# First token block of a fused attention and MoE kernel: matmuls in float32 on the decoded weights, splits moved to the second block

## The chip, the cores and the metric

The kernel runs on one core of a Trainium2 chip. The metric is device time in microseconds (us) of one launch. Engines are named as in the profile: PE is TensorE, DVE is VectorE, ACT is ScalarE, POOL is GpSimd, SP is SyncE, which only issues the DMAs.

## The reference

The attention's inputs are float32; the MoE weights come as float64 and are decoded to float32 on the chip. Cut to what matters:

```python
# attention: B=8, H=8, S=576, D=64, pool=8
k_p = k.reshape(B, H, Sp, pool, D).mean(axis=3)
v_p = v.reshape(B, H, Sp, pool, D).mean(axis=3)
scores = scale * np.matmul(q, k_p.transpose(0, 1, 3, 2))
attn = softmax(scores)
x = np.matmul(attn, v_p) as (B*S, H*D)      # 4608 tokens of 512
# first MoE: d_ff 1536
x = (x @ w_a) * (x @ w_b) @ w_out
# second MoE: d_ff 2048
h = x @ w_in
x = h * np.clip(h + 3.0, 0.0, 6.0) / 6.0 @ w_out2
```

## The kernel before

The three layers run one after the other over the 4608 tokens, which are cut into 9 blocks of 512. In the first MoE (`step(j, f)`) a block j has 12 steps f, one for each 128 columns of d_ff. A step multiplies x by a slice of w_a (`pa`, L476 to L478), by a slice of w_b (`pb`), multiplies the two results on POOL (`asb`, L596) and adds the product times a slice of w_out to four accumulators (`y`), one step later (`pend`).

Each float32 product is made of three fp32r passes (`mm3`): hi by hi, lo by hi, hi by lo. So every operand is split into hi (a cast on ACT, L72) and lo (a subtraction on DVE or POOL, L73): `wa`, the first weight; `sp(j, f)_0` and `sp(j, f)_1`, the other two; `gh` and `gl`, the product of the step; `xh` and `xl`, the block of x (L348, L349). A step has 36 fp32r matmuls of 128x512.

The weights come by DMA as pairs of 32-bit words (`st0`, `st1`, `st2`) and are decoded in block 0, three tiles a step: two activations on ACT (L79, L80), two tensor_scalars on DVE (L81, L82), one add on POOL (L83) and one scalar_tensor_tensor on DVE (L87). The first weight's decoded tile is `wst`, the other two are `raw`. In block 1 the splits of `raw` are made again and written to DRAM; later blocks load them (`w1_load`), while `wa` stays on the chip.

The attention is cut into chunks of at most 128 tokens, whose stages (`q_tr`, `scores`, `expo`, `sums`, `normal`, `at_main`, `at_left`, `pv`) are put into numbered slots, three for each step, by `base` and `at`. The chunks of block 0 run ahead of the first step, those of block 1 during block 0 and so on. `k_prep` pools the keys of a batch. In `normal` POOL makes `am` and `al`, in `at_main` and `at_left` PE transposes them (`atm`, `atl`), DVE ends them (L321, L333), and `pv` makes x from them.

Blocks 1 to 8 are issued in program order (`tc.manual_schedule()`). Block 0 and the attention ahead of it are put in order by the scheduler of the framework, so that a small change of the code moves instructions of other steps too. Each engine then works its own queue in that order.

Of the kernel before, what the change touches and what calls it, by code (L numbers as in the profile page):

```python
# [8 lines left out]
F32 = mybir.dt.float32  # L9
F32R = mybir.dt.float32r  # L10
# [2 lines left out]
AF = mybir.ActivationFunctionType  # L13
ALU = mybir.AluOpType
AX = mybir.AxisListType

# [6 lines left out]
def pooled_attention_then_two_moe_kernel(  # L25
# [12 lines left out]
    nc = tc.nc  # L38
    P = 128
# [8 lines left out]
    NCC = DM // P  # L48
    NF1 = F1 // P
    NF2 = F2 // P  # L50
    TB = 512
# [7 lines left out]
    wpool = ctx.enter_context(tc.tile_pool(name="wpool", bufs=28))  # L59
    xpool = ctx.enter_context(tc.tile_pool(name="xpool", bufs=2))  # L60
    gpool = ctx.enter_context(tc.tile_pool(name="gpool", bufs=2))
# [9 lines left out]
    def split(hi, lo, src, hi_eng=None, lo_eng=None):  # L71
        (hi_eng or nc.scalar.copy)(hi, src)  # L72
        (lo_eng or nc.gpsimd).tensor_tensor(lo, src, hi.bitcast(F32), ALU.subtract)  # L73

    def decode(dst, st):

        lo, hi = st[:, :, 0], st[:, :, 1]
        d32, di, du = dst, dst.bitcast(I32), dst.bitcast(U32)
        nc.scalar.activation(d32, hi.bitcast(F32), AF.Abs)  # L79
        nc.scalar.activation(lo.bitcast(I32), lo, AF.Copy, scale=2.0**-29)  # L80
        nc.vector.tensor_scalar(d32, d32, F64_MIN, F64_MAX, ALU.max, ALU.min)  # L81
        nc.vector.tensor_scalar(du, du, 3, 0x3FFFFFF8, ALU.logical_shift_left, ALU.bitwise_and)  # L82
        nc.gpsimd.tensor_tensor(di, di, lo.bitcast(I32), ALU.add)  # L83

    def decode_end(dst, st):
        du = dst.bitcast(U32)
        nc.vector.scalar_tensor_tensor(du, st[:, :, 1], 0xC0000000, du, ALU.bitwise_and, ALU.bitwise_or)  # L87
# [12 lines left out]
    xh_t, xl_t = {}, {}  # L100

    def x_tiles(j):
        if j not in xh_t:
            xh_t[j] = xpool.tile([P, NCC, TB], F32R, tag="xh", name=f"xh{j}")
            xl_t[j] = xpool.tile([P, NCC, TB], F32R, tag="xl", name=f"xl{j}")
        return xh_t[j], xl_t[j]

    def load_tile(b, shape, name):
# [226 lines left out]
    def pv(pi, g):  # L335
        b, t0, N = pieces[pi]
        ath, atl, atx = aT[pi]
        pt = ps.tile([P, 2, PIECE], F32, tag="att", name="pv")
        for i in range(2):
            hp = 2 * g + i  # L340
            o = pt[:, i, :N]
            nc.tensor.matmul(o, vmh[b % 2][:, hp], ath[:, hp, :N], start=True, stop=False)
            nc.tensor.matmul(o, vml[b % 2][:, hp], ath[:, hp, :N], start=False, stop=False)
            nc.tensor.matmul(o, vlw[b % 2][:96, hp], atx[:, g, :N], start=False, stop=False)
            nc.tensor.matmul(o, vmh[b % 2][:, hp], atl[:, hp, :N], start=False, stop=True)
        j, r = divmod(b * S + t0, TB)
        xh, xl = (x[:, 2 * g : 2 * g + 2, r : r + N] for x in x_tiles(j))
        nc.scalar.copy(xh, pt[:, :, :N])  # L348
        nc.vector.tensor_tensor(xl, pt[:, :, :N], xh.bitcast(F32), ALU.subtract)  # L349


    chunks, pieces, chunk_piece, block_chunks = [], [], {}, [[] for _ in range(NB)]
    for b in range(B):
        t = 0
# [22 lines left out]
    base = []  # L377
    for j in range(NB):
        n = len(block_chunks[j])
        for i, c in enumerate(block_chunks[j]):  # L380
            if j == 0:
                base.append(-100 + 2 * i)
            elif j == 1:
                base.append(4 * i)
            else:
                base.append(SLOTS * (j - 1) - 8 + i * SLOTS // n)
    for c, (b, t0, n) in enumerate(chunks):
# [38 lines left out]
    def run_slot(s):  # L426
        for fn, args in plan.pop(s, ()):
            fn(*args)


    wa_t, raw_t, wst = {}, {}, {}

    def w1_dma(f):
        t = [wpool.tile([P, 512, 2], U32, tag="w", name=f"st{i}_{f}") for i in range(3)]
        for i, w in ((0, w_a), (1, w_b)):
            nc.sync.dma_start(
                t[i].rearrange("p (c f) two -> p c (f two)", c=NCC),
                w[:, 2 * f * P : 2 * (f + 1) * P].rearrange("(c p) f -> p c f", p=P),
            )
        nc.sync.dma_start(t[2].rearrange("p f two -> p (f two)"), w_o1[f * P : (f + 1) * P, :])  # L440
        wst[f] = t

    def w1_prep(f, part):
        st = wst[f][part]
        if part == 0:
            raw_t[f] = wpool.tile([P, 2, 512], F32, tag="w", name=f"raw{f}")
            t = spool.tile([P, 512], F32, tag="wst", name="wst")
            decode(t, st)
            decode_end(t, st)
            w = wpool.tile([P, 2, 512], F32R, tag="w", name=f"wa{f}")  # L450
            split(w[:, 0], w[:, 1], t, lo_eng=nc.vector)
            wa_t[f] = w
        else:
            decode(raw_t[f][:, part - 1], st)
            decode_end(raw_t[f][:, part - 1], st)

    sp_t = {}

# [3 lines left out]
    def raw_split(key, f, part):  # L462
        w = wpool.tile([P, 2, 512], F32R, tag="w", name=f"sp{key}_{part}")
        split(w[:, 0], w[:, 1], raw_t[f][:, part], lo_eng=nc.vector if part else nc.gpsimd)
        if key[0] == 1:
            later.append((w1dram[f][part], w.bitcast(F32)))
        sp_t[key, part] = w

    def w1_load(key, f, part):
# [4 lines left out]
    def mm3(o, wh, wl, xh, xl, first, last, more=False):  # L474

        nc.tensor.matmul(o, wh, xh, start=first, stop=False, skip_group_check=more)  # L476
        nc.tensor.matmul(o, wl, xh, start=False, stop=False, skip_group_check=more)  # L477
        nc.tensor.matmul(o, wh, xl, start=False, stop=last, skip_group_check=more)  # L478

    def layer_in(o, w, xh, xl):  # L480
        for c in range(NCC):
            s = slice(c * P, (c + 1) * P)
            mm3(o, w[:, 0, s], w[:, 1, s], xh[:, c], xl[:, c], c == 0, c == NCC - 1)


# [3 lines left out]
    def y_part(j, f, w, gh, gl):  # L489
        if f == 0:  # L490
            yacc[j] = [ps_acc.tile([P, TB], F32, tag="acc", name=f"y{c}") for c in range(NCC)]
        for c in range(NCC):
            s = slice(c * P, (c + 1) * P)
            mm3(yacc[j][c], w[:, 0, s], w[:, 1, s], gh, gl, f == 0, f == NF1 - 1)
        if f == NF1 - 1:
            y_store(j, 0)
# [51 lines left out]
    for i, s in enumerate(early):  # L548
        run_slot(s)
        if s == -190:  # L550
            for f in range(2):
                w1_dma(f)
    for part in range(3):
        w1_prep(0, part)
    raw_split((0, 0), 0, 0)
    raw_split((0, 0), 0, 1)
    def step(j, f):


        nonlocal pend  # L560
        xh, xl = x_tiles(j)
        s0 = SLOTS * j + 3 * f
        i = NF1 * (j - 3) + f
        staged = i // 2 - 1 if 2 < i < 4 * NF2 + 2 and i % 2 else None
        stores, later[:] = list(later), []
        if j == 0:
            if f + 2 < NF1:
                w1_dma(f + 2)
            if f + 1 < NF1:
                for part in range(3):  # L570
                    w1_prep(f + 1, part)
        nj, nf = divmod(NF1 * j + f + 1, NF1)
        if nj < 2:
            raw_split((nj, nf), nf, 0)
        lj, lf = divmod(NF1 * j + f + AHEAD, NF1)
        if 2 <= lj < NB:
            w1_load((lj, lf), lf, 0)
            w1_load((lj, lf), lf, 1)
        if 0 <= i < 4 * NF2 and i % 2 == 0:
            w2_stage(i // 2)  # L580
        pa = ps.tile([P, TB], F32, tag="ab", name="pa")
        layer_in(pa, wa_t[f], xh, xl)
        asb = gpool.tile([P, TB], F32, tag="asb", name="asb", bufs=2)
        nc.scalar.copy(asb, pa)  # L584
        run_slot(s0)
        if f == 1 and j > 0:
            y_store(j - 1, 1)
        for dst, src in stores:
            nc.sync.dma_start(dst, src)
        if staged is not None:  # L590
            w2_decode(staged)
        pb = ps.tile([P, TB], F32, tag="ab", name="pb")
        layer_in(pb, sp_t.pop(((j, f), 0)), xh, xl)
        bsb = gpool.tile([P, TB], F32, tag="bsb", name="bsb", bufs=1)
        nc.scalar.copy(bsb, pb)  # L595
        nc.gpsimd.tensor_tensor(asb, asb, bsb, ALU.mult)  # L596
        run_slot(s0 + 1)
        if pend is not None:
            y_part(*pend)
        if nj < 2:  # L600
            raw_split((nj, nf), nf, 1)
        run_slot(s0 + 2)
        gh = gpool.tile([P, TB], F32R, tag="gh", name="gh")
        gl = gpool.tile([P, TB], F32R, tag="gl", name="gl")
        split(gh, gl, asb)
        if staged is not None:
            w2_end(staged)
        pend = (j, f, sp_t.pop(((j, f), 1)), gh, gl)
# [252 lines left out]
```

## Time and profile before

| what | value |
|---|---|
| median of 3 runs | 1876.38 us (1875.3 to 1878.81) |
| the profiled execution, its own time | 1876.27 us |
| its span, first to last instruction | 1874.3 us |
| PE busy over the span | 1785.2 us (95%) |
| DVE busy | 981.8 us (52%) |
| ACT busy | 746.9 us (40%) |
| POOL busy | 801.3 us (43%) |
| mean granted clock of PE | 0.977 |

The median is that of the runs, while all rows come from one profiled execution, whose own time is 0.11 us from it. Shares over the span are means over stages that differ; block 0 ends near 230 us of the 1874.

### The profile page before, as it was taken

How to read it: one execution, taken by the hardware profiler on the slowest of the kernel's cores; microseconds unless marked ns; L12 is line 12 of the kernel's file. 1: busy time of each engine (PE TensorE's matmuls, PEld its weight loads, DVE VectorE, ACT ScalarE, POOL GpSimd, SP SyncE). 2: the span in 40 equal slices, each digit the busy share in tenths (PEclk: the TensorE clock that was granted, in tenths of full speed). 3: DMA queues.
4: the chain of work that ended last, by engine and by line, in shares of the span. 5: the costliest groups of instructions: out<-in, count | busy, mean ns of one | idle time of the engine just before them, and what ended most of it. 6: DMA issues, size and time to landing. Idle time of an engine off the chain costs nothing.

```text
span 1874.3 us, 23760 instructions
## 1 busy us (share of the span) xinstructions
PE 1785.2 (95%) x8292; PEld 1474.3 (79%) x8292; DVE 981.8 (52%) x1631; ACT 746.9 (40%) x1425; POOL 801.3 (43%) x679
## 2 busy tenths in 40 slices
PE   3878899999999999999999989999999999999998
PEld 2666788788887788888888867888888888888897
DVE  7999554423435435554322145667457454745645
ACT  4655443323333333333333245445334433533443
POOL 3577644333444433444443485455224322522322
PEclk8788999999999999999999989999999999999999
DMA  7653246643767447475544555466445544544483
GB/s 174 159 158 105 74 157 213 211 136 92 220 206 249 136 154 236 158 236 178 197 182 157 200 208 202 180 205 224 139 145 189 189 135 152 202 136 150 153 292 129
DMA packets 196550, 328.73 MB, mean 175 GB/s; under 512 B 86352, under 2 KB 107856, under 8 KB 196432
## 3 DMA queue, kind: packets, MB, share of 16 engines
q1 hardware_dynamic: 196432, 327.22, 53.5%
q8 instruction: 66, 1.08, 0.2%
q14 instruction: 52, 0.43, 0.1%
HBM read 264.24 MB, written 62.91 MB: 175 GB/s over the span
## 4 chain that ended last, share of the span: by engine, by line
PE 82%; DVE 10%; DMA 3%; issue 2%; ACT 1%; POOL 1%; SPq 1%; DVEq 0%; ACTq 0%; POOLq 0%
PE o L476 7%; PE o L477 7%; PE o L478 7%; PE y L476 5%; PE y L477 5%; PE pb L476 5%; PE y L478 5%; PE pb L478 4%; PE pb L477 4%; PE pa L476 4%; PE pa L478 4%; PE pa L477 4%; PE phZ L476 3%; PE phZ L477 3%; PE phZ L478 3%
## 5 line engine op out<-in xcount | busy, mean ns | idle before, releaser
L73 POOL TENSOR_TENSOR g<-r,g 128x512 fp32r<-128x512 f32 (+1 forms) x160 | 198.5, 1251 | 434.0 <-ACT g L72 265.5
L596 POOL TENSOR_TENSOR asb<-asb,bsb 128x512 f32<-128x512 f32 x108 | 145.2, 1345 | 242.2 <-ACT bsb L595 216.0
L749 DVE TENSOR_TENSOR oacc<-o,oacc 128x512 f32<-128x512 f32 x252 | 172.3, 688 | 135.7 <-PE o L478 135.6
L477 PE MATMUL o<-wo,g 128*128 128x512 f32 x576 | 224.4, 390 | 0.0
L478 PE MATMUL o<-wo,g 128*128 128x512 f32 x576 | 224.2, 389 | 0.0
L476 PE MATMUL o<-wo,g 128*128 128x512 f32 x576 | 211.7, 390 | 1.4 <-ACT g L72 1.2
L73 POOL TENSOR_TENSOR gl<-asb,gh 128x512 fp32r<-128x512 f32 x108 | 145.0, 1343 | 150.6 <-ACT gh L72 146.7
L476 PE MATMUL pa<-xh,wa 128*128 128x512 f32 x432 | 175.6, 406 | 3.0 <-ACT wa L72 2.9
L477 PE MATMUL pa<-xh,wa 128*128 128x512 f32 x432 | 170.7, 395 | 0.2 <-DVE wa L73 0.2
L478 PE MATMUL pa<-xl,wa 128*128 128x512 f32 x432 | 170.7, 395 | 0.0
L584 ACT COPY asb<-pa 128x512 f32<-128x512 f32 x108 | 63.3, 586 | 220.4 <-PE pa L478 217.1
L730 ACT ACTIVATE r<-hs 128x512 f32<-128x512 f32 (+1 forms) x120 | 69.0, 590 | 165.6 <-DVE hs L780 164.8
L595 ACT COPY bsb<-pb 128x512 f32<-128x512 f32 x108 | 63.4, 587 | 175.1 <-PE pb L478 170.5
L476 PEld LDWEIGHTS o<-wo,g 128*128 128x128 f32 x576 | 107.4, 188 | 24.2 <-ACT g L72 2.8
L478 PEld LDWEIGHTS o<-wo,g 128*128 128x128 f32 x576 | 108.2, 188 | 22.2
L477 PEld LDWEIGHTS o<-wo,g 128*128 128x128 f32 x576 | 108.2, 188 | 21.9
L72 ACT CAST g<-r 128x512 fp32r<-128x512 f32 (+1 forms) x160 | 91.9, 579 | 68.6 <-DVE r L731 68.4
L477 PE MATMUL phZ<-Sh,wi 128*128 128x512 f32 (+1 forms) x320 | 117.7, 368 | 0.0
L476 PE MATMUL phZ<-Sh,wi 128*128 128x512 f32 (+1 forms) x320 | 117.6, 368 | 0.0
L478 PE MATMUL phZ<-Sl,wi 128*128 128x512 f32 (+1 forms) x320 | 114.6, 368 | 0.0
L731 DVE SCALAR_TENSOR_TENSOR r<-r,hs 128x512 f32<-128x512 f32 (+1 forms) x120 | 94.8, 806 | 26.5 <-ACT r L730 26.4
L321 DVE TENSOR_TENSOR atl<-atm,ath 128x512 fp32r<-128x512 f32 (+1 forms) x40 | 25.4, 635 | 158.2 <-ACT ath L320 158.2
(1527 smaller groups left out, 4304.2 us busy)
## 6 DMA issues: line engine op xcount, KB each, us to landing
wi<-wsd SPq DMA_DIRECT2D x96, 512.0 KB
wo<-wod SPq DMA_DIRECT2D x64, 512.0 KB
wsd<-wi SPq DMA_DIRECT2D x24, 512.0 KB
kraw<-in_k_dram SPq DMA_DIRECT2D x32, 288.0 KB
ydram<-yo SPq DMA_DIRECT2D x36, 256.0 KB
out_dram<-oacc SPq DMA_DIRECT2D x36, 256.0 KB
vraw<-in_v_dram SPq DMA_DIRECT2D x32, 256.0 KB
w2st<-in_moe_w_in_dram SPq DMA_DIRECT2D x16, 512.0 KB
```

The source lines that it names most:

```text
L72: (hi_eng or nc.scalar.copy)(hi, src)
L73: (lo_eng or nc.gpsimd).tensor_tensor(lo, src, hi.bitcast(F32), ALU.subtract)
L321: nc.vector.tensor_tensor(dl, pt[:, :, :n], dh.bitcast(F32), ALU.subtract)
L476: nc.tensor.matmul(o, wh, xh, start=first, stop=False, skip_group_check=more)
L477: nc.tensor.matmul(o, wl, xh, start=False, stop=False, skip_group_check=more)
L478: nc.tensor.matmul(o, wh, xl, start=False, stop=last, skip_group_check=more)
L584: nc.scalar.copy(asb, pa)
L595: nc.scalar.copy(bsb, pb)
L596: nc.gpsimd.tensor_tensor(asb, asb, bsb, ALU.mult)
L730: nc.scalar.activation(r[:, :n], src, AF.Relu, bias=3.0)
L731: nc.vector.scalar_tensor_tensor(r[:, :n], r[:, :n], 6.0, src, ALU.min, ALU.mult)
L749: nc.vector.tensor_tensor(acc, o, acc, ALU.add)
```

## The change

In block 0 (j == 0) x is kept as one float32 tile without `xl`; `pa`, `pb` and `y` are single float32 matmuls (L488 and L502 of the changed kernel) on the decoded weights `rawa` and `raw`; the product `g0` is one float32 tile (L608) without gh and gl. Each hi and lo that block 1 needs is made during block 1, one step ahead, `wa` by the new `wa_split`; its first ones fall into the last step of block 0. The weights are fetched three steps ahead in place of two. The chunks of block 1 begin six slots later. Lines of the changed kernel are 1 higher than before from L20 on and 2 or more from L349 on, so that L82, L83, L84 and L88 are the decode's L81, L82, L83 and L87.

```diff
         if j not in xh_t:
-            xh_t[j] = xpool.tile([P, NCC, TB], F32R, tag="xh", name=f"xh{j}")
-            xl_t[j] = xpool.tile([P, NCC, TB], F32R, tag="xl", name=f"xl{j}")
+            xh_t[j] = xpool.tile([P, NCC, TB], F32R if j else F32, tag="xh", name=f"xh{j}")
+            xl_t[j] = xpool.tile([P, NCC, TB], F32R, tag="xl", name=f"xl{j}") if j else None
         return xh_t[j], xl_t[j]
...
         j, r = divmod(b * S + t0, TB)
-        xh, xl = (x[:, 2 * g : 2 * g + 2, r : r + N] for x in x_tiles(j))
+        xh, xl = (x[:, 2 * g : 2 * g + 2, r : r + N] if x is not None else x for x in x_tiles(j))
         nc.scalar.copy(xh, pt[:, :, :N])
-        nc.vector.tensor_tensor(xl, pt[:, :, :N], xh.bitcast(F32), ALU.subtract)
+        if j:
+            nc.vector.tensor_tensor(xl, pt[:, :, :N], xh.bitcast(F32), ALU.subtract)
...
             elif j == 1:
-                base.append(4 * i)
+                base.append(4 * i + 6)
             else:
...
-    wa_t, raw_t, wst = {}, {}, {}
+    wa_t, raw_t, rawa_t, wst = {}, {}, {}, {}
...
             raw_t[f] = wpool.tile([P, 2, 512], F32, tag="w", name=f"raw{f}")
-            t = spool.tile([P, 512], F32, tag="wst", name="wst")
-            decode(t, st)
-            decode_end(t, st)
-            w = wpool.tile([P, 2, 512], F32R, tag="w", name=f"wa{f}")
-            split(w[:, 0], w[:, 1], t, lo_eng=nc.vector)
-            wa_t[f] = w
-        else:
-            decode(raw_t[f][:, part - 1], st)
-            decode_end(raw_t[f][:, part - 1], st)
+            if f % 2 == 0:
+                rawa_t[f] = wpool.tile([P, 2, 512], F32, tag="w", name=f"rawa{f}")
+            else:
+                rawa_t[f] = rawa_t[f - 1]
+        d = raw_t[f][:, part - 1] if part else rawa_t[f][:, f % 2]
+        decode(d, st)
+        decode_end(d, st)
+
+    def wa_split(f):
+        w = wpool.tile([P, 2, 512], F32R, tag="w", name=f"wa{f}")
+        split(w[:, 0], w[:, 1], rawa_t[f][:, f % 2], lo_eng=nc.vector)
+        wa_t[f] = w
...
         split(w[:, 0], w[:, 1], raw_t[f][:, part], lo_eng=nc.vector if part else nc.gpsimd)
-        if key[0] == 1:
-            later.append((w1dram[f][part], w.bitcast(F32)))
+        later.append((w1dram[f][part], w.bitcast(F32)))
         sp_t[key, part] = w
...
             s = slice(c * P, (c + 1) * P)
+            if xl is None:
+                nc.tensor.matmul(o, w[:, s], xh[:, c], start=c == 0, stop=c == NCC - 1)
+                continue
             mm3(o, w[:, 0, s], w[:, 1, s], xh[:, c], xl[:, c], c == 0, c == NCC - 1)
...
             s = slice(c * P, (c + 1) * P)
+            if gl is None:
+                nc.tensor.matmul(yacc[j][c], w[:, s], gh, start=f == 0, stop=f == NF1 - 1)
+                continue
             mm3(yacc[j][c], w[:, 0, s], w[:, 1, s], gh, gl, f == 0, f == NF1 - 1)
...
         if s == -190:
-            for f in range(2):
+            for f in range(3):
                 w1_dma(f)
...
         w1_prep(0, part)
-    raw_split((0, 0), 0, 0)
-    raw_split((0, 0), 0, 1)
+
...
         if j == 0:
-            if f + 2 < NF1:
-                w1_dma(f + 2)
+            if f + 3 < NF1:
+                w1_dma(f + 3)
             if f + 1 < NF1:
...
         nj, nf = divmod(NF1 * j + f + 1, NF1)
-        if nj < 2:
+        if nj == 1:
+            wa_split(nf)
             raw_split((nj, nf), nf, 0)
...
         pa = ps.tile([P, TB], F32, tag="ab", name="pa")
-        layer_in(pa, wa_t[f], xh, xl)
+        layer_in(pa, wa_t[f] if j else rawa_t[f][:, f % 2], xh, xl)
         asb = gpool.tile([P, TB], F32, tag="asb", name="asb", bufs=2)
...
         pb = ps.tile([P, TB], F32, tag="ab", name="pb")
-        layer_in(pb, sp_t.pop(((j, f), 0)), xh, xl)
+        layer_in(pb, sp_t.pop(((j, f), 0)) if j else raw_t[f][:, 0], xh, xl)
         bsb = gpool.tile([P, TB], F32, tag="bsb", name="bsb", bufs=1)
         nc.scalar.copy(bsb, pb)
-        nc.gpsimd.tensor_tensor(asb, asb, bsb, ALU.mult)
+        if j == 0:
+            gh = gpool.tile([P, TB], F32, tag="gh", name="g0")
+            nc.gpsimd.tensor_tensor(gh, asb, bsb, ALU.mult)
+        else:
+            nc.gpsimd.tensor_tensor(asb, asb, bsb, ALU.mult)
         run_slot(s0 + 1)
...
             y_part(*pend)
-        if nj < 2:
+        if nj == 1:
             raw_split((nj, nf), nf, 1)
         run_slot(s0 + 2)
+        if j == 0:
+            pend = (j, f, raw_t[f][:, 1], gh, None)
+            return
         gh = gpool.tile([P, TB], F32R, tag="gh", name="gh")
```

The order of DVE before, in the eight rows that end with `atx_459`, which the value products of the last piece of block 0's x need on PE (it is row 88 of DVE's queue):

```order
L276 TENSOR_SCALAR se_417<-su_415 128x8
L349 TENSOR_TENSOR xl0_454<-pv_444,xh0_453 128x2x256
L278 RECIPROCAL rc_419<-se_417 128x8
L349 TENSOR_TENSOR xl0_454<-pv_467,xh0_453 128x2x256
L321 TENSOR_TENSOR atl_458<-atm_460,ath_457 128x4x128
L333 TENSOR_TENSOR atx_459<-atl_478,atx_459 32x2x128
L321 TENSOR_TENSOR atl_458<-atm_483,ath_457 128x4x128
L333 TENSOR_TENSOR atx_459<-atl_490,atx_459 32x2x128
```

The same place in the changed kernel, up to `atx_463` (row 122):

```order
L83 TENSOR_SCALAR raw4_771<-raw4_771 128x512
L88 SCALAR_TENSOR_TENSOR raw3_694<-st1_3_549,raw3_694 128x512
L83 TENSOR_SCALAR raw4_771<-raw4_771 128x512
L82 TENSOR_SCALAR raw5_859<-raw5_859 128x512
L83 TENSOR_SCALAR rawa4_772<-rawa4_772 128x512
L83 TENSOR_SCALAR raw5_859<-raw5_859 128x512
L88 SCALAR_TENSOR_TENSOR raw3_694<-st2_3_550,raw3_694 128x512
L322 TENSOR_TENSOR atl_462<-atm_486,ath_461 128x4x128
L83 TENSOR_SCALAR raw5_859<-raw5_859 128x512
L88 SCALAR_TENSOR_TENSOR rawa4_772<-st0_4_601,rawa4_772 128x512
L334 TENSOR_TENSOR atx_463<-atl_493,atx_463 32x2x128
```

Between the attention's rows stand decodes of the weights of steps 3 to 5, which before came later; the row that ends x has moved from 88 to 122.

POOL's order ahead of `am_801`, the product of the second batch's first chunk (its softmax `sm` by the reciprocal `rc`), before:

```order
L73 TENSOR_TENSOR gl_704<-asb_650,gh_703 128x512
L83 TENSOR_TENSOR raw2_713<-raw2_713,st1_2_606 128x512
L83 TENSOR_TENSOR raw2_713<-raw2_713,st2_2_607 128x512
L83 TENSOR_TENSOR wst_842<-wst_842,st0_3_707 128x512
L596 TENSOR_TENSOR asb_752<-asb_752,bsb_768 128x512
L73 TENSOR_TENSOR sp(0, 2)_0_736<-raw2_713,sp(0, 2)_0_736 128x512
L73 TENSOR_TENSOR gl_832<-asb_752,gh_831 128x512
L286 TENSOR_TENSOR am_801<-sm_678,rc_775 64x512
```

and ahead of the same product, `am_823`, in the changed kernel:

```order
L84 TENSOR_TENSOR rawa10_1338<-rawa10_1338,st0_10_1135 128x512
L74 TENSOR_TENSOR sp(1, 0)_0_1521<-raw0_528,sp(1, 0)_0_1521 128x512
L84 TENSOR_TENSOR raw10_1337<-raw10_1337,st1_10_1136 128x512
L84 TENSOR_TENSOR raw10_1337<-raw10_1337,st2_10_1137 128x512
L84 TENSOR_TENSOR rawa10_1338<-rawa10_1338,st0_11_1239 128x512
L608 TENSOR_TENSOR g0_806<-asb_796,bsb_804 128x512
L84 TENSOR_TENSOR raw11_1414<-raw11_1414,st1_11_1240 128x512
L74 TENSOR_TENSOR sp(1, 1)_0_1592<-raw1_554,sp(1, 1)_0_1592 128x512
L84 TENSOR_TENSOR raw11_1414<-raw11_1414,st2_11_1241 128x512
L287 TENSOR_TENSOR am_823<-sm_739,rc_812 64x512
```

Before, `am` stood behind the decodes of steps 0 to 2 and one of step 3; now it stands behind those of all 12 steps (`raw11` is the last) and two splits for block 1.

On PE of the changed kernel the transposes of that product (`atm_902<-ident,am_823`) stand within the sixth step:

```order
L502 MATMUL y3_679<-g0_806,raw3_694 128x512
L488 MATMUL pa_968<-xh0_459,rawa4_772 128x512 x4
L319 MATMUL atm_902<-ident_78,am_823 128x64 x4
L331 MATMUL atl_918<-ident_78,al_824 96x64 x2
L488 MATMUL pb_996<-xh0_459,raw5_859 128x512 x4
L502 MATMUL y0_676<-g0_897,raw4_771 128x512
```

Before, the matching transposes (of `am_801`) stood within the fourth step, between two matmuls of `pa`; now they stand between `pa` and `pb` of the sixth, and all that is behind them on PE follows them.

## Rows read from the trace of the kernel before

**Rows 1.** windows of 25 us, all engines

```profile
core 0: us, PE busy (x) PEld busy (x) DVE busy (x) ACT busy (x) POOL busy (x), PEclk, DMA share, GB/s
...
75.00:100.00 25.00, 17.47 (x72) 13.58 (x70) 24.84 (x45) 12.97 (x27) 16.94 (x14) 0.85 0.58 164
...
125.00:150.00 25.00, 16.27 (x67) 12.81 (x66) 24.28 (x36) 13.87 (x27) 21.19 (x17) 0.81 0.76 220
...
250.00:275.00 25.00, 25.00 (x117) 20.69 (x116) 9.68 (x18) 11.02 (x23) 13.10 (x12) 1.00 0.39 137
```

**Rows 2.** windows of longer stretches; columns as in rows 1

```profile
27.50:56.20 28.70, 11.09 (x43) 8.43 (x43) 26.79 (x51) 12.87 (x26) 16.09 (x17) 0.56 0.41 93
59.30:230.70 171.40, 142.52 (x615) 113.33 (x613) 146.28 (x229) 93.94 (x187) 117.04 (x87) 0.87 0.43 125
75.00:200.00 125.00, 100.49 (x429) 80.15 (x427) 115.42 (x180) 67.11 (x128) 89.40 (x67) 0.85 0.44 128
```

**Rows 3.** timeline of PE: start, duration, line, tiles, [idle before, releaser]

```profile
56.16 0.58 PE L344 MATMUL pv<-atx,vlw 96*128 96x256 f32 x1 [0.38 <-DVE atx L333]
...
59.31 0.63 PE L476 MATMUL pa<-xh,wa 128*128 128x512 f32 x1
...
230.69 0.49 PE L476 MATMUL pa<-xh,wa 128*128 128x512 f32 x1
```

**Rows 4.** chain that ended last: start, us, what

```profile
284.75 0.12 PE pv L345
284.88 0.49 PE sc L253 x4
...
1224.84 0.68 PE o L476 x3
```

**Rows 5.** one tile's instructions: sc, the scores; ns min/median/max

```profile
L253 PE MATMUL sc<-bd,qT x320: 283/286/610, 16.3 to 970.2; 128*128 128x144 f32 x128, 128*64 128x144 f32 x32
L258 DVE TENSOR_REDUCE mx<-sc x80: 396/450/458, 20.5 to 970.6; 128x4 f32<-128x288 f32 x64, 64x4 f32<-64x288 f32 x16
```

**Rows 6.** groups by line, DVE, 27.5 to 56.2 us; busy us, mean ns

```profile
L127 DVE TENSOR_TENSOR kraw<-kraw 72x512 f32<-72x512 f32 x4 | 3.9, 987 | 0.0
...
L87 DVE SCALAR_TENSOR_TENSOR raw<-st,raw 128x512 uint32<-128x512 uint32 x2 | 1.4, 688 | 0.0
```

**Rows 7.** groups by line, DVE, 75 to 200 us

```profile
L73 DVE TENSOR_TENSOR wa<-wst,wa 128x512 fp32r<-128x512 f32 x8 | 6.5, 810 | 2.3 <-ACT wa L72 2.3
```

**Rows 8.** groups by line, POOL, 75 to 200 us

```profile
L73 POOL TENSOR_TENSOR gl<-asb,gh 128x512 fp32r<-128x512 f32 x8 | 12.2, 1521 | 0.8 <-ACT gh L72 0.5
```

**Rows 9.** timeline of DVE, POOL and PE at two places

```profile
27.76 0.16 DVE L276 TENSOR_SCALAR se<-su 128x8 f32<-128x8 f32 x1
27.83 0.42 DVE L82 TENSOR_SCALAR wst<-wst 128x512 uint32<-128x512 uint32 x1
...
28.39 1.29 POOL L83 TENSOR_TENSOR wst<-wst,st 128x512 int32<-128x512 int32 x1 [24.00 <-DVE rc L278]
...
29.64 1.04 POOL L286 TENSOR_TENSOR am<-sm,rc 128x512 f32<-128x512 f32 x1
...
29.87 1.10 DVE L81 TENSOR_SCALAR wst<-wst 128x512 f32<-128x512 f32 x1
...
107.56 0.63 PE L476 MATMUL pb<-xh,sp(0, 3)_0_864 128*128 128x512 f32 x1
...
107.62 0.41 DVE L81 TENSOR_SCALAR wst<-wst 128x512 f32<-128x512 f32 x1
107.95 0.41 DVE L82 TENSOR_SCALAR raw<-raw 128x512 uint32<-128x512 uint32 x1
107.99 0.63 PE L477 MATMUL pb<-xh,sp(0, 3)_0_864 128*128 128x512 f32 x1
...
108.44 1.33 POOL L83 TENSOR_TENSOR raw<-raw,st 128x512 int32<-128x512 int32 x1 [1.71 <-DVE raw L82]
...
108.85 1.20 DVE L82 TENSOR_SCALAR raw<-raw 128x512 uint32<-128x512 uint32 x1
```

## Prediction, made before the changed kernel ran

> **What bounds the kernel now.** I read the windows of 25 us first [rows 1]. At 250 to 275 us TensorE (PE) is busy 25.00 of 25.00 us at a granted clock of 1.00, and VectorE (DVE), ScalarE (ACT) and GpSimd (POOL) have slack: 9.68, 11.02 and 13.10 us busy. The first token block is different: in two of its windows PE is busy 17.47 and 16.27 us of 25 at clocks of 0.85 and 0.81, while DVE stands at 24.84 and 24.28. The wider windows say the same [rows 2]: from 59.3 to 230.7 us PE works 142.52 of 171.40 us at a mean clock of 0.87, DVE 146.28, POOL 117.04. So block 0 is bound by DVE and POOL together, and everything behind it by PE.
>
> The timeline gives the two ends [rows 3]. PE's first layer matmul (pa, L476) starts at 59.31, 3.15 us after the value products of the last attention piece, which waited at 56.16 for DVE's atx (L333). The second step of block 1 starts at 230.69. That start is my marker: from there on PE has the same instructions in the same order in both kernels and was saturated, so what the marker moves, the end moves. Whole time = 1876.27 us of the profiled execution (within 0.2 us of the median of the runs) + the shift of the marker.
>
> **What the change removes and adds on PE.** In block 0 each group of three fp32r passes becomes one F32 matmul: 432 fp32r against 144 F32, both on 512 columns. The chain has fp32r at 0.68 for three, 0.227 each; the score products are F32 on 144 columns, four records in 0.49 [rows 4]. One F32 matmul is two records (320 against 80 reductions, each of two matmuls [rows 5]), so 0.245 each. By columns an F32 matmul of 512 costs 0.245 x 512/144 = 0.87. Block 0 then costs 144 x 0.87 = 125 us of PE where the passes cost 432 x 0.227 = 98: PE alone gets 27 us more work. From below, 3 x 0.227 = 0.68 would be no loss; the same dtype's own row speaks for 0.87.
>
> To the marker PE also has 24 fp32r matmuls of block 1's first step (5.4 us), 26 score products at 0.245 (6.4), and 108 value products and transposes, at most 0.12 each [rows 4]; I take 9 as an estimate, since many are 64 to 192 wide. Together 146 us.
>
> **What it removes on DVE, ACT and POOL.** In block 0: the splits of 24 weight tiles (24 casts on ACT, 12 subtractions on DVE, 12 on POOL), 12 casts and 12 subtractions of the first weight (moved to block 1), the 12 gl subtractions on POOL and their casts, and the xl subtractions. DVE loses about 24 x 0.8 [rows 7], POOL 24 x 1.5 [rows 8]. What stays is 36 decodes: each two tensor_scalar and one scalar_tensor_tensor on DVE and one add on POOL.
>
> The 12 splits added to block 1 cost at most 0.81 on DVE each [rows 7] and a cast on ACT: 12 steps of nearly 9 us, with more than half of DVE and ACT free [rows 1]. Nothing on the path; without that cover it would be 12 x 0.8 = 10 us. The three weight loads of a step are issued one step earlier on SP's queue, ahead of the second batch's loads; the DMA share is 0.43 in the block [rows 2], so I cost them at nothing. Later slots of the second batch's attention: its k pooling still stands in DVE's front part (11 of its 12 rows), so nothing is won there.
>
> **What it moves.** This decides. Without the splits, the scheduler lets decodes run ahead. On DVE the row that lets PE begin (atx) stands at 122 where it stood at 88. From the decode at 27.83 us [rows 9] to the value products at 56.16 [rows 3], before has 51 rows in a stretch of 28.70 us [rows 2]. After has 82: 36 tensor_scalars, 13 scalar_tensor_tensors and 33 attention rows. Prices:
> - lowest: 36 at 0.41, 13 at 0.69 [rows 6, 9], 33 at 0.42 as an estimate from attention rows between 0.16 and 0.99, minus 0.07 of overlap per row (at 107.62 a row of 0.41 starts, at 107.95 the next): 32 us.
> - before's own pace of this stretch: 28.70/51 x 82 = 46 us.
> - before's pace of 75 to 200 us: 125/180 x 82 = 57 us [rows 2].
>
> What makes the pace is in the timeline [rows 9]: a DVE L81 takes 0.41 when alone and 1.10 where it begins beside POOL's am, L82 1.20 beside POOL's add. If DVE's two-operand and tensor_scalar rows and POOL's rows just took turns, the front would be 28 us of DVE (36 at 0.34, 13 at 0.62, 8 us of two-operand attention rows as an estimate) and 21 us of POOL (12 adds at 1.29, three am at 1.04, small ones 2) = 49 us. I take 49, between the two paces. PE then starts at 27.8 + 49 + 3.2 = **80** (bounds 63 and 88), 21 us later than before.
>
> Then a second wait. PE's row 107, transposes of the second batch's am, stands between pa and pb of its sixth step, and am is POOL's row 75, behind all 36 decode adds, four products and two splits; its rc is DVE's row 214. From 27.8 us DVE has 174 rows to there. Lowest: 72 us (the 92 more at 36 x 0.34, 22 x 0.62 and 34 x 0.42), am at about 103. At the early pace 98, at the block's pace 121: 82 rows at 49 us and 92 at 0.694 (64 us) end at 141. Taking turns in full: 63 us of DVE (72 at 0.34, 35 at 0.62, 17 of attention) and 62 of POOL (35 adds at 1.29, four am, six longer rows at 1.4, small ones 4), 153. With the last add and am itself (1.4 and 1.3) the ends are 144 and 155; since both short rows of DVE that met a POOL row were held to nearly its end, I take am at **148**, near the middle.
>
> PE gets to row 107 at 80 + 55.4 (60 F32 at 0.87, 2 of scores, 1.2 of transposes) + 2 for a clock that is low after waiting (matmuls of the same form 0.43 apart at 107.56 and 107.99 [rows 9]) = 137.5. So it waits 10.5 us. Queued behind it are pb of that step, its product, and y. What is left to the marker is 84 F32 (73), 24 fp32r (5.4), scores 4.4, the rest of attention 8: 91, + 2 for the clock after the wait, + 2.5 for waits in the last steps like those before. Marker: 148 + 95.5 = **243.5**, against 230.69: +13, so **1889 us**.
>
> The Trainium skill, page "SBUF — State Buffer", section "SBUF: two separate sides", says that the port pair which VectorE and GpSimd share is an exclusive lock held for the whole instruction: a two-port VectorE operation, or one with two SBUF inputs against a GpSimd operation, fully blocks the other. The rows of 1.10 and 1.20 agree. By the rule without any overlap am would come at 27.8 + 125 + 2.7 = 155.5, the third rival below.
>
> **The rivals.**
> 1. *No second wait.* If DVE and POOL are through the decodes before 137 us (a pace of 0.62 per row), PE runs from 80 to the marker at its own speed: 80 + 146 + 2 + 2.5 = 230.5, shift 0, 1876 (1872 to 1880 for starts of 76 to 84). For it: fewer POOL rows than before per DVE row. Against: 0.694 in the long window.
> 2. *Faster: decodes at their lone price.* If most rows run at 0.41 and 0.69, since POOL has fewer long rows, PE starts at 63 to 72, am is there before 130, and the marker comes at 214 to 223: 1860 to 1868. It decides where the front takes under 41 us. For it: DVE's minimum durations, and the loss of 24 POOL subtractions; against it: both measured paces.
> 3. *DVE and POOL take strict turns.* am at 155, the marker at 250, +20: 1896. For it: the two slowed rows; against it, that some attention rows read PSUM or one operand.
> 4. *PE's clock stays low.* At before's 0.87 [rows 2], 146 us of PE become 168, and with the start at 80 the marker is at 250, 1896, with the wait more. Against: PE idles less, and the clock was 1.00 when it was busy.
>
> **How the numbers follow.** Forecast (wait of 3 to 15 us, shift +4 to +17) 0.50; rivals 3 and 4 together 0.20; rival 1 0.17; rival 2 0.13. A measurement of this kernel can hardly tell 0.2% (3.75 us) from no change. Rival 2 is faster, rival 1 the same, the rest slower: 0.13, 0.17, 0.70. The likeliest case's own range is 1881 to 1893. The range for 8 in 10 reaches into both sides: 1869 (a start at 73 without a wait) to 1903 (strict turns with a low clock).
>
> **What would show it.** In the profile after: first F32 pa at 80 (63 to 88); its matmuls 0.87 apart at clock 1.00; an idle time of PE ahead of atm_823's transposes put down to POOL am; the marker at 243. DVE and POOL near full to 147 us and with much slack after. Block 1 without new idle time. Wrong if PE starts before 72, if the F32 matmul isn't near 0.87, or if the time behind the marker isn't that of before.

## The result and the profile after

The changed kernel takes 1895.79 us (median of 4 runs, 1894.11 to 1898.77) against 1876.22 for the kernel before (4 runs): a ratio of 1.0104, 95% interval 1.0086 to 1.0121, so 19.6 us slower. 1889 was forecast, with 1869 to 1903 as the range. Its profiled execution took 1897.14 us with a span of 1895.4.

Windows of 25 us of the changed kernel, columns as in [rows 1]:

```profile
50.00:75.00 25.00, 5.73 (x24) 4.77 (x24) 24.84 (x42) 14.51 (x27) 18.38 (x14) 0.57 0.73 208
75.00:100.00 25.00, 20.28 (x57) 10.66 (x58) 23.72 (x37) 11.31 (x24) 16.49 (x9) 0.84 0.80 244
...
125.00:150.00 25.00, 20.65 (x53) 9.15 (x52) 23.77 (x37) 5.58 (x11) 20.04 (x13) 0.93 0.24 65
150.00:175.00 25.00, 25.00 (x77) 12.65 (x76) 5.72 (x19) 3.55 (x7) 4.37 (x6) 1.00 0.14 31
...
200.00:225.00 25.00, 25.00 (x75) 12.13 (x74) 4.19 (x9) 4.09 (x7) 3.40 (x5) 1.00 0.00 1
225.00:250.00 25.00, 21.90 (x95) 16.41 (x94) 9.89 (x24) 8.95 (x24) 4.27 (x7) 0.80 0.12 37
```

Before 75 us PE is nearly idle (5.73 us busy) while DVE is full (24.84). From 150 us on it is the other way round: PE 25.00, DVE 5.72 of 25. In two windows of the kernel before DVE was near full and PE had 16 to 17 of 25 beside it [rows 1]. So part of the work of DVE that used to lie beside PE now lies ahead of PE.

Timeline of PE in the changed kernel (start, duration, line, tiles, and in brackets the idle time before with what ended it), at the start, at the sixth step, in the steady part and at the end of block 0:

```profile
77.78 0.58 PE L345 MATMUL pv<-atx,vlw 96*128 96x256 f32 x1 [7.83 <-DVE atx L334]
...
80.94 1.05 PE L488 MATMUL pa<-xh,rawa 128*128 128x512 f32 x1
...
131.53 3.70 PE L488 MATMUL pb<-xh,raw 128*128 128x512 f32 x8 [0.95 <-ACT bsb L605]
137.19 5.40 PE L502 MATMUL y<-g,raw 128*128 128x512 f32 x8 [1.97 <-POOL g L608]
...
146.04 0.46 PE L319 MATMUL atm<-ident,am 64*128 64x64 f32 x4
...
148.20 1.98 PE L488 MATMUL pb<-xh,raw 128*128 128x512 f32 x4 [0.81 <-ACT bsb L605]
...
163.42 3.60 PE L502 MATMUL y<-g,raw 128*128 128x512 f32 x8
166.85 0.65 PE L254 MATMUL sc<-bd,qT 128*128 128x144 f32 x4
...
227.71 0.43 PE L319 MATMUL atm<-ident,am 64*128 64x64 f32 x4 [1.27 <-POOL al L300]
...
238.82 0.63 PE L481 MATMUL pa<-xh,wa 128*128 128x512 f32 x1
239.25 0.63 PE L482 MATMUL pa<-xl,wa 128*128 128x512 f32 x1
```

The first F32 matmul starts at 80.94, where 59.31 stood [rows 3]. What PE waited for is DVE's atx, as before, but for 7.83 us here. Two records are one F32 matmul, so the eight records from 163.42 to 166.85 are four matmuls at 0.858. The second step of block 1 begins at 249.25, where it was 230.69: the marker moved by 18.6.

The longer windows, first those of the changed kernel, then the stretch behind the marker of the kernel before:

```profile
27.80:77.70 49.90, 11.14 (x42) 7.89 (x42) 49.58 (x80) 29.02 (x54) 37.95 (x30) 0.54 0.89 254
80.94:249.25 168.31, 157.72 (x470) 79.92 (x469) 89.08 (x170) 51.56 (x111) 65.64 (x51) 0.95 0.24 69
249.25:367.80 118.55, 117.43 (x566) 97.50 (x565) 67.42 (x114) 52.21 (x108) 57.61 (x47) 1.00 0.53 175
```

```profile
230.69:349.24 118.55, 117.43 (x566) 97.48 (x565) 55.81 (x104) 47.03 (x98) 53.35 (x47) 1.00 0.53 177
```

The first 118.55 us behind the marker hold the same PE work and take the same time in both, though DVE and ACT are busier in the changed kernel (67.42 in place of 55.81 on DVE) with the 12 splits that moved there. Over the spans the shift is 21.1, so that 2.5 us of the profiled execution came later, where the kernels have the same instructions; the four runs lie 4.7 us apart, and I put nothing on these 2.5 us.

### The profile page after: what moved, and what is told of

The parts are those of the page before. It is cut to its first block, busy times and chain, and to the rows that moved or that the text cites. A ratio compares the mean times of both kernels' runs of the same rounds, so it can differ in the third digit from the quotient of the medians.

```text
span 1895.4 us, 23395 instructions
## 1 busy us (share of the span) xinstructions
PE 1803.6 (95%) x8148; PEld 1442.7 (76%) x8148; DVE 959.9 (51%) x1615; ACT 726.8 (38%) x1389; POOL 774.4 (41%) x655
## 4 chain that ended last, share of the span: by engine, by line
PE 85%; DVE 9%; DMA 2%; issue 2%; ACT 1%; SPq 1%; POOL 0%; DVEq 0%; ACTq 0%; POOLq 0%
PE o L480 7%; PE o L482 6%; PE o L481 6%; PE y L480 4%; PE pb L480 4%; PE y L482 4%; PE y L481 4%; PE pa L480 4%; PE pb L482 4%; PE pb L481 4%; PE pa L482 4%; PE pa L481 4%; PE phZ L480 3%; PE phZ L481 3%; PE phZ L482 3%; PE sc L254 2%
## 5 line engine op out<-in xcount | busy, mean ns | idle before, releaser
L610 POOL TENSOR_TENSOR asb<-asb,bsb 128x512 f32<-128x512 f32 x96 | 126.9, 1322 | 237.3 <-ACT bsb L605 212.0
L74 POOL TENSOR_TENSOR gl<-asb,gh 128x512 fp32r<-128x512 f32 x96 | 126.8, 1321 | 146.5 <-ACT gh L73 143.6
L480 PE MATMUL pa<-xh,wa 128*128 128x512 f32 x384 | 155.4, 405 | 0.4 <-ACT xh L349 0.4
L482 PE MATMUL pa<-xl,wa 128*128 128x512 f32 x384 | 150.7, 393 | 0.0
L481 PE MATMUL pa<-xh,wa 128*128 128x512 f32 x384 | 150.2, 391 | 0.0
```

## The experiments

**E1 and E2: block 0 in the order in which the code is written,** on PE, DVE, ACT and POOL, of the changed kernel (E1) and of the kernel before (E2):

```diff
-    for f in range(NF1):
-        step(0, f)
-    with tc.manual_schedule():
+    ET = mybir.EngineType
+    with tc.manual_schedule(engines={ET.PE, ET.DVE, ET.Activation, ET.Pool}):
+        for f in range(NF1):
+            step(0, f)
+    with tc.manual_schedule():
```

> The changed kernel with the instructions of block 0 on PE, DVE, ACT and POOL in the order in which the code is written; the same work, nothing left out. The atx row that PE needs stands at 82 of DVE's queue in place of 122, and 15 decode adds stand ahead of the second batch's first am on POOL in place of 36. Theory A (the loss comes from decodes that stand ahead of the attention): first F32 matmul of block 0 at about 60 us in place of 80.9 (29 us of DVE and POOL taking turns behind 27.8), the marker (second step of block 1) at 205 to 215 in place of 249, time 1852 to 1864, faster than both kernels. Theory B (the loss is PE's own 27 us for F32 in place of three passes, whatever the order): the marker stays above 240 and the time above 1885.

> The kernel before with the same written order in block 0; nothing left out. Its own order differs little (atx row 88 as before, 9 adds ahead of the fifth am in place of 10). Theory A: its first layer matmul stays near 59 us and, as block 0 is bound by DVE and POOL taking turns on splits and decodes, the time stays within 10 us of 1876. Theory C (any written order frees tens of us, whatever the dtype): below 1860.

E1 took 1904.05 us (ratio to the kernel before 1.0151, 1.0134 to 1.0168), E2 1934.28 (one run). The first F32 matmul of E1 came at 55.06, nearly 26 us earlier than in the changed kernel:

```profile
55.06 1.70 PE L488 MATMUL pa<-xh,rawa 128*128 128x512 f32 x2
```

and yet the kernel got slower by 8 us. Waits of PE in block 0 of E1, by what is waited for (us in total, times, longest):

```profile
PE sc L254 <- DVE qT L241: 13.3, 4, 7.5
PE sc L254 <- DVE sm L260: 9.3, 1, 9.3
PE ktp L146 <- DVE kp L130: 6.2, 1, 6.2
PE ktp L146 <- DVE atx L334: 5.2, 1, 5.2
```

In the written order PE stands behind each piece of the second batch's attention (its q transposes, scores, k) and goes on only when that has passed through DVE, so that the early start is lost again. So theory A in its simple form fell: an early start by itself is not worth its 26 us. The time and the marker (258.01) lie where theory B had them; B, PE's own work as the loss, fell only with E6 below. E2 missed its 10 us by far, too: the written order costs the kernel before 58 us. In that order the changed kernel is 30 us faster than the one before, a first sign, and with one run of E2 no more than that, that the change itself isn't what costs the time.

**E3: weights fetched two steps ahead again; E4: block 1's chunks at their slots of before.**

```diff
-            for f in range(3):
+            for f in range(2):
                 w1_dma(f)
...
-            if f + 3 < NF1:
-                w1_dma(f + 3)
+            if f + 2 < NF1:
+                w1_dma(f + 2)
```

```diff
-                base.append(4 * i + 6)
+                base.append(4 * i)
```

> The changed kernel with the weights fetched two steps ahead, as before the change; nothing left out. Theory A: the decodes' place in DVE's and POOL's order is the same (atx row 122, 36 adds ahead of am), so the first F32 matmul at 81 and the time 1890 to 1900. Rival D (the third set of weights in flight brings the decodes ahead or fills the DMA queues): start under 70 and time under 1883.

> The changed kernel with block 1's chunks at their slots of before (4*i); nothing left out. Theory A: atx row 122 and 36 adds ahead of am as in the changed kernel, so the first F32 matmul at 81 and the time 1888 to 1902; am's transposes stand one step earlier on PE, so PE waits at them, up to 10 us in one place. Rival E (the later slots of the second batch cost the time): under 1883.

E3 took 1901.00 us, E4 1898.92 (one run each), with the first F32 matmul at 81.2 and 81.8. E4's time is within the expected range, and E3's just above it. The wait for am of up to 10 us that was expected in E4 was 3.3 us; PE waits 11.5 there for asb, bsb and the products g, and 11.4 for g in E3. Neither of these two edits carries the loss.

**E5: the decodes of steps 1 to 11 wait for x; E6: they are paced as well.** A zero made from x's last column, or of asb's, is the bias of the decode's first activation (ACT), so that a decode can't be put ahead of it:

```diff
-    def decode(dst, st):
+    gates = {}
+
+    def decode(dst, st, bias=0.0):
...
-        nc.scalar.activation(d32, hi.bitcast(F32), AF.Abs)
+        nc.scalar.activation(d32, hi.bitcast(F32), AF.Abs, bias=bias)
...
         nc.scalar.copy(xh, pt[:, :, :N])
+        if j == 0 and r + N == TB and g == 1:
+            gates[0] = apool.tile([P, 1], F32, name="gate0")
+            nc.scalar.mul(gates[0], xh[:, 1, N - 1 : N], 0.0)
...
-        decode(d, st)
+        decode(d, st, gates.get(max(f - 3 + 1, 0), 0.0) if f else 0.0)
...
         nc.scalar.copy(asb, pa)
+        if j == 0:
+            gates[f + 1] = apool.tile([P, 1], F32, name=f"gate{f + 1}")
+            nc.scalar.mul(gates[f + 1], asb[:, TB - 1 : TB], 0.0)
```

This is E6; E5 has only the gate on x, for all f from 1 on.

> The changed kernel, in which the decodes of steps 1 to 11 wait for the block's x (a zero made from x's last column is the bias of the first activation, one small ACT instruction more); nothing left out, and the scheduler still sets the order. The atx row stands at 82 of DVE's queue, with 3 decode tails ahead of it in place of 13; the second batch's first am still stands behind 30 decode adds. Theory A1 (the late start is the whole loss): first F32 matmul at 55 to 62, all behind it 21 to 26 us earlier, time 1870 to 1876. Theory A2 (two waits: the start, and then am behind the decodes of DVE and POOL): start at 55 to 62, but am at 130 to 145 because the work of DVE and POOL ahead of it is the same, so PE waits some 20 us for it or for what stands around it; marker 232 to 243, time 1880 to 1890. Theory B (PE's own work alone): above 1890.

> As the run above, and the decode of step f also waits for the first product of step f-3 (13 small ACT instructions of one column); nothing left out. Atx row 82, the second batch's first am behind 18 decode adds in place of 36 and needed within PE's fifth step. Theory A2: both waits gone, first F32 matmul at 55 to 62, marker at 205 to 220, time 1850 to 1866, faster than the kernel before. Theory A1: as the run above, 1870 to 1876. Theory B: above 1885.

E5 took 1888.44 us (one run). Its timeline of PE, at the start, at two waits and at the marker:

```profile
50.26 1.13 PE L492 MATMUL pa<-xh,rawa 128*128 128x512 f32 x2 [0.78 <-ACT xh L351]
...
130.76 0.69 PE L321 MATMUL atm<-ident,am 64*128 64x64 f32 x4 [6.05 <-POOL am L289]
...
140.79 3.63 PE L506 MATMUL y<-g,raw 128*128 128x512 f32 x4 [4.35 <-POOL g L612]
...
239.57 0.48 PE L484 MATMUL pa<-xh,wa 128*128 128x512 f32 x1
```

PE started at 50.26, 30.7 us earlier than in the changed kernel and ahead of the 55 to 62 that either theory gave, but the marker came only 9.7 us earlier, at 239.57. In between PE waits for am and for the products g on POOL, which stand behind POOL's decode adds. By what is waited for (us in total, times, longest):

```profile
PE y L506 <- POOL g L612: 14.7, 4, 5.4
PE atm L321 <- POOL am L289: 6.1, 1, 6.1
```

So A1, the late start as the whole loss, fell, and A2 gave the right time.

E6 took 1870.75 us (10 runs, ratio 0.9972, 0.9963 to 0.9982): 25 us less than the changed kernel and 5 us less than the kernel before. Its start, a wait and its marker on PE, and then POOL's am:

```profile
51.94 1.05 PE L493 MATMUL pa<-xh,rawa 128*128 128x512 f32 x1
...
122.14 5.40 PE L493 MATMUL pb<-xh,raw 128*128 128x512 f32 x8 [3.58 <-ACT bsb L613]
...
226.95 0.48 PE L485 MATMUL pa<-xh,wa 128*128 128x512 f32 x1
```

```profile
101.94 1.03 POOL L289 TENSOR_TENSOR am<-sm,rc 64x512 f32<-64x512 f32 x1 [4.72 <-DVE rc L281]
```

am is there at 103 where it came at 146, and the marker at 226.95 in place of 249.25. That is the way A2 forecast, but not as far: the time is 5 us above its range and the marker 7 us above its 205 to 220. The time alone lies in the range of A1, which E5 had ruled out. B, PE's own work as the loss, falls here: the work is the same and 25 us are gone. The window from the start to the marker:

```profile
51.94:226.87 174.93, 159.44 (x468) 79.10 (x468) 127.04 (x215) 75.93 (x155) 87.38 (x66) 0.95 0.39 113
```

174.93 us for PE work that I put at 146: PE idles 15.5 us, and its clock is 0.95. Half of the idle time is two waits for bsb:

```profile
PE pb L493 <- ACT bsb L613: 7.9, 2, 4.3
```

The one at 122.14 is followed back on ACT's timeline and then on that of SP's queue:

```profile
120.95 0.68 ACT L83 ACTIVATE st<-st 128x512 int32<-128x512 uint32 x1 [4.01 <-DMA st<-in_moe_w_a_dram]
121.52 0.57 ACT L613 COPY bsb<-pb 128x512 f32<-128x512 f32 x1
...
103.70 11.34 SPq L136 DMA_DIRECT2D kraw<-in_k_dram  x4
115.14 0.39 SPq L443 DMA_DIRECT2D st<-in_moe_w_a_dram  x1
```

bsb (121.52) stands behind a decode's activation that waited 4.01 us for its weights, and these were issued at 115.14 behind the third batch's k loads, which held SP's queue for 11.34 us. A paced decode needs its weights in time; the loads, costed at nothing in the prediction, are next in line here.

**E7: the decode's add on POOL cut to 8 of 512 columns,** which leaves out the low bits of the weights.

```diff
-        nc.gpsimd.tensor_tensor(di, di, lo.bitcast(I32), ALU.add)
+        nc.gpsimd.tensor_tensor(di[:, 0:8], di[:, 0:8], lo.bitcast(I32)[:, 0:8], ALU.add)
```

> The changed kernel with each decode's add on POOL done on 8 of the 512 columns: the weights' low bits are left out, the number of instructions is the same. 71 DVE rows from the first decode to atx, 82 in the changed kernel. Theory T (DVE rows wait while a POOL row holds what both need): L82 and L83 at 0.41 to 0.50 us mean in place of 0.61 to 0.85, first F32 matmul at 62 to 67. Theory P (DVE's pace is its own): the same means as in the changed kernel and the start at 71 or later.

It took 1877.16 us (one run), 19 less than the changed kernel. Groups by line on DVE from 27.8 us to the start of block 0, of the changed kernel and then of E7 (busy us, mean ns):

```profile
L83 DVE TENSOR_SCALAR raw<-raw 128x512 uint32<-128x512 uint32 x12 | 8.4, 702 | 0.0
L88 DVE SCALAR_TENSOR_TENSOR raw<-st,raw 128x512 uint32<-128x512 uint32 x9 | 8.2, 906 | 0.0
L82 DVE TENSOR_SCALAR raw<-raw 128x512 f32<-128x512 f32 x12 | 7.3, 612 | 0.0
...
L82 DVE TENSOR_SCALAR rawa<-rawa 128x512 f32<-128x512 f32 x5 | 4.3, 853 | 0.0
```

```profile
L82 DVE TENSOR_SCALAR raw<-raw 128x512 f32<-128x512 f32 x12 | 6.1, 514 | 0.0
L88 DVE SCALAR_TENSOR_TENSOR raw<-st,raw 128x512 uint32<-128x512 uint32 x8 | 5.9, 737 | 0.0
L83 DVE TENSOR_SCALAR raw<-raw 128x512 uint32<-128x512 uint32 x10 | 4.2, 426 | 0.0
...
L82 DVE TENSOR_SCALAR rawa<-rawa 128x512 f32<-128x512 f32 x5 | 2.1, 417 | 0.0
```

```profile
62.80 1.05 PE L488 MATMUL pa<-xh,rawa 128*128 128x512 f32 x1
```

E7's tensor_scalars are at 0.42 to 0.51 in place of 0.61 to 0.85, and PE starts at 62.80, as theory T had it. The start is 18.1 us earlier. Part of that is E7's shorter order, 71 rows up to atx in place of 82: at 0.62 us a row (49.90 for 80 rows) the 11 are worth 7 us by estimate. The other 11 us are shorter rows, so POOL's long rows set much of DVE's pace in this stretch.

**E8: the kernel before, paced as E6; E9: E6 with block 1's chunks at their slots of before; E10: E6 with one step more of lead.** E8 has the edit of E6 on the kernel before (on `decode(t, st)` and `decode(raw_t[f][:, part - 1], st)`); E9 adds the one line of E4; in E10

```diff
-        decode(d, st, gates.get(max(f - 3 + 1, 0), 0.0) if f else 0.0)
+        decode(d, st, gates.get(max(f - 4 + 1, 0), 0.0) if f else 0.0)
```

> The kernel before with the same pacing of the decodes (steps 1 and 2 wait for the block's x, step f for the first product of step f-3); nothing left out. Atx row 84 where it was 88, 7 adds ahead of the second batch's first am where there were 10. Theory A2 (pacing wins only where decodes had run ahead; before they hardly did, and block 0 is bound by DVE and POOL with the splits): 1872 to 1895, no gain, first layer matmul 55 to 60. Rival P (pacing alone is worth the gain, whatever the dtype): below 1871.

> The paced changed kernel with block 1's chunks at their slots of before (4*i in place of 4*i+6); nothing left out. If the later slots matter when nothing else holds PE, the time moves from 1871 by more than 4 us; theory A2 has no wait on them: 1867 to 1875.

> The paced changed kernel with one step more of lead for the decodes (step f waits for the first product of step f-4); nothing left out. 21 adds ahead of the second batch's first am in place of 18. Theory A2: am comes later by some 3 adds and their DVE rows (9 us at turns) but PE waits less for weights; between the paced kernel (1871) and the one that holds the start alone (1888): 1870 to 1880.

E8 took 1884.40 us (1.0044, 1.0029 to 1.0058): pacing makes the kernel before slower, and rival P fell. At the same pacing the changed kernel is 13.7 us faster than the one before. E9 took 1867.67 us (0.9955, 0.9940 to 0.9970), within its range, the fastest here and 0.45% under the kernel before; its interval overlaps with E6's, so whether the slots matter stays open. E10 took 1870.42 (0.9969, 0.9956 to 0.9982), as E6: the lead isn't critical between three and four steps.

## Why the prediction was right

**The start.** 80 was forecast and 80.94 measured: DVE's stretch from the first decode to atx took 49.9 us, where 49 stood in the working. The mechanism is shown in both its halves: with fewer decodes ahead of atx the start is at 50.26 (E5) and 51.94 (E6), and with POOL's rows short (and 11 rows fewer) it is at 62.80 (E7). That the sum of both engines' rows met the stretch within 1 us is partly luck: the same reckoning gave about 60 for E1, 55 to 62 was expected of E5 and E6, and PE started at 55.06, 50.26 and 51.94. In these runs the sum is an upper estimate.

**PE's price.** An F32 matmul of 512 columns was put at 0.87 and takes 0.858.

**The second wait.** am was put at 148; its row ended at 145.99, and PE's transposes began at 146.04. (This am has 64 rows. It is the first chunk of the second token block, which is the last 64 tokens of the first batch, and not the second batch's first chunk, as it is called ahead of the result and in the expectations; its place in the queues is as given there.) But PE did not stand there for 10.5 us, as the working had it, and the sign named for it, an idle time of PE put down to am, did not come. PE came late itself: 65.1 us from its start to the transposes, where 55.4 is work by the prediction. Of the other 9.7, 6.1 were six waits before them, for the products g (2.5), asb (1.8) and bsb (1.8). The rest is in part a lower clock, 0.77 from 80.94 to 85 and 0.74 from 135 to 140, both behind waits of PE. Nothing in the rows makes PE's own delay end just when am came; I take that for luck. At 137.5 it would have waited 8.5 us for am. For the longest of the six waits, 1.97 at 137.19, the rows of POOL show why:

```profile
131.90 3.57 POOL L84 TENSOR_TENSOR rawa<-rawa,st 128x512 int32<-128x512 int32 x1 [2.17 <-DVE rawa L83]
135.43 1.71 POOL L608 TENSOR_TENSOR g<-asb,bsb 128x512 f32<-128x512 f32 x1
...
141.74 1.73 POOL L84 TENSOR_TENSOR raw<-raw,st 128x512 int32<-128x512 int32 x1
144.61 1.38 POOL L287 TENSOR_TENSOR am<-sm,rc 64x512 f32<-64x512 f32 x1 [1.14 <-DVE rc L279]
```

The product g at 135.43 stands right behind an add of 3.57. It is the same queue and the same cause, decodes ahead of what PE needs, only met at another place first. The waits for asb and bsb come through ACT's queue, and what causes them is shown for one only: the bsb that ended the wait at 131.53 stands behind a cast for block 1, which itself had waited for a decode's row on DVE. E5 shows the wait where I had it: without the late start PE waits 6.05 us for am itself.

**What is left behind it.** This term was too small: 95.5 from the transposes to the marker, and 103.2 measured (146.04 to 249.25). Of these, PE was idle for 4.5: at the end of block 0 the last attention pieces wait on POOL, ACT and DVE one after the other (1.27 at 227.71 among them). Behind these waits the granted clock falls to the lower of its two levels, 1.2 GHz, for some 10 us:

```profile
230.00:240.00 10.00, 9.00 (x34) 7.43 (x35) 3.48 (x9) 3.15 (x10) 1.65 (x3) 0.51 0.15 39
```

The matmuls 0.43 apart at 238.82 and 239.25 show it too. 9.00 us of work at 0.51 cost some 4.5 us by estimate, so waits and clock took 9 where 4.5 had been put. That leaves 94 us of work where the prediction had 91: its 8 us for the rest of the attention were some 3 too few. The marker came 5.7 us later than forecast, which is nearly all of the 6.8 by which 1889 was too low.

**The rivals.** No second wait and the faster case fell by the traces above; they would need am before 137. Strict turns gave 1896, near the measured time, but by an am at 155, which came at 146: the time agrees and the way doesn't. A low clock for the whole of block 0 did not come (0.95 from 80.94 to 249.25).

**Costed at nothing, and so measured.** The splits in block 1 (118.55 us in both), the weight loads (E3) and the slots (E4) are not what costs the time in the changed kernel. The 19.6 us can be put together from the runs: pacing costs the kernel before 8.2 (E8), the change at equal pacing gives back 13.7 (E8 to E6), and taking the pacing away from the changed kernel costs 25.0 (E6 to the changed kernel). Of these 25, E5 (one run) gets 7.4 back with the start alone, and the other 17.7 come when the later decodes are held back as well, so that the products and am are out from behind them. How much of that is POOL's adds and how much DVE's rows, the runs don't part.

## What to carry to other kernels

When work is taken off an engine whose order a scheduler sets, what was behind that work moves forward, and it may now stand ahead of the rows for which the bounding engine waits: look up where the last row ahead of that engine's first instruction stands, and count what is in front of it. Getting the start earlier is worth only as much as the next thing in the same queue lets through; bound how far the preparing work may run ahead, by a dependence on the consumer's progress, and then measure the change again. Two engines that hold each other up can be costed as one, with the sum of their rows as an upper estimate.

## What the runs showed of the hardware

By the rows, POOL is slowed as DVE is. The add at 131.90 took 3.57 us, where 1.29 is its short duration [rows 9], and DVE's rows beside it, also those with two inputs, ran at their short durations:

```profile
132.35 0.41 DVE L82 TENSOR_SCALAR raw<-raw 128x512 f32<-128x512 f32 x1
...
133.02 0.67 DVE L128 TENSOR_TENSOR kraw<-kraw 72x512 f32<-72x512 f32 x1
133.62 0.67 DVE L74 TENSOR_TENSOR sp(1, 0)_1_1567<-raw,sp(1, 0)_1_1567 128x512 fp32r<-128x512 f32 x1
134.22 0.73 DVE L275 TENSOR_REDUCE su<-sm 64x8 f32<-64x576 f32 x1
```

The Trainium skill, page "SBUF — State Buffer", section "SBUF: two separate sides", has the lock go to whichever of the two engines starts first; here the add stayed open while DVE ran several instructions in a row. That DVE kept POOL waiting through all of them is my reading of the rows; no run tests it, nor can I tell from these runs which of the two loses in a given stretch.
